# Sums of seven-product blocks ended in PSUM, and weight and word preparation moved between engines

## The chip, the core and the metric

The kernel runs on one core of one Trainium2 chip. The metric is device time in microseconds (us) of one execution. Before the change it is 1180.49 us, the median of three runs (1179.92, 1180.49 and 1183.63).

The names of the engines: PE is the matrix engine, DVE is VectorE, ACT is ScalarE, POOL is GpSimd, and SP is SyncE, which here issues nearly all DMAs. PSUM holds the results of matrix products in banks of 128x512 fp32 values, and SBUF everything else.

## The reference

Attention over 4 batches of 576 tokens, with 8 heads of 64, then two feed-forward blocks, all in float32:

```python
scores = (q_rot @ k_rot.T) / sqrt(64); attn = softmax(scores)
x = concat_heads(attn @ v)                                # 2304 x 512
x = (silu(x @ w_gate) * (x @ w_val)) @ w_out              # MoE1, d_ff 1536
out = (relu(x @ w_in2) ** 2) @ w_out2                     # MoE2, d_ff 2048
```

`q_rot` and `k_rot` are rotated by their positions. The weights arrive as 64-bit floats and are used with float32 accuracy.

## The kernel before

**Products.** Every matrix product is made of three products of rounded operands: each operand is split into a high part (ACT, L873, or a DVE cast) and the rest, its low part (a subtraction on POOL or DVE, L874), and PE adds high·high, high·low and low·high in PSUM (L1020). What the text calls a split is this pair of instructions.

**Tokens.** Each batch has 576 tokens. 512 of them form a block; the 64 left over of all four batches form a fifth block, the rest, of 256 tokens. Batches are worked in two pairs, (0,1) and (2,3).

**Seven products for eight.** For a pair, the up projections (gate, val, and `w_in2`) treat tokens and d_ff columns as a 2x2 block product and compute it with seven products (function `up`). They need seven words of the tokens (B11, T1, T2, B22, T3, B21, T4; the T words are differences of the batches) and seven weights of a 256-column group (four parts and four sums or differences, `combine`). Each of the seven products of one group is six 128x512 matmuls. Three partial results are copied from PSUM to SBUF by ACT (tiles `cp`), and three later ones are added to them by DVE into the SBUF tile (`cp<-q,cp`). The four results (1,1), (0,1), (0,0) and (1,0) then pass through the activation: in MoE1 a DVE instruction multiplies with the gate (`th<-th,cp`), in MoE2 one computes max(x,0)·x in place (`cp<-cp`). Each result is then split into a tile `h`, which the down projection (`down`) multiplies with `wo`; DVE adds its output to the accumulators (`acc<-d,acc`).

**Stages.** First attention, with the first two d_ff chunks of MoE1 of batches 0 to 2 as filler for PE (L780; outputs go through a tile `ys` to a buffer `ypart` in device memory, L807 and L808). Its end is also the start of the first two chunks of block 3 and the rest (`glu0`). Then MoE1 in five groups of 256 d_ff columns, for pair 0 with the rest, then for pair 1; then MoE2 in eight groups for pair 0 with the rest, and for pair 1. `down` is run once for each of these 26 groups.

**Weights.** A group's weights are loaded as 64-bit words (L378) and unpacked in `unpack`: ACT scales the high word, DVE shifts the low word (L893), and two DVE instructions with a shift and an OR (L881) build the fp32 word. In the feed-forward blocks all of these write SBUF tiles (`raw`, then `f` or `wf`). In the attention the same three instructions go through a PSUM tile `mm` (L384 to L386). `combine` makes the weight sums, four DVE instructions of 128x256 each (`f<-f`), and writes the group to device memory for pair 1. Then come the splits into `wi` and `wo`.

**Words.** Those of the first pair are made after the attention: tokens are read back from `xfull` (L870), DVE makes the differences (`tw`), and all seven words are split into the `xc` tiles. The words of the later pairs are written to device memory, read back by `fetch_x` and split.

**Order of the work.** Attention and filler are ordered by class `Plan` with rank numbers. The rest is listed in program order with the functions `dma`, `split`, `tt`, `stt`, `copy` and `mul` (L869 to L1023), and class `Order` (L214) schedules it: PE takes its products in the written order, every other instruction has a due time counted back from PE, and an engine takes the most urgent instruction that is ready in the plan. Where an instruction may run on two engines (a `split` with `free=True`), the plan chooses. The resulting order of each engine is fixed in the program. Buffers are rings of tiles of fixed length (`Ring`).

Of the kernel before, what the change touches and what calls it, by code (L numbers as in the profile page):

```python
# [213 lines left out]
class Order:  # L214


    HOP = 200
    LAND = 2000
    RATE = 310
    WINDOW = 4  # L220

# [3 lines left out]
    def add(self, ways, rd=(), wr=(), size=0):  # L225
# [28 lines left out]
        self.ops.append(dict(ways=ways, deps=deps, at=at, now=self.pe, size=size, stage=self.stage))  # L254

    def plan(self):
# [19 lines left out]
        free = dict.fromkeys(ready, True)  # L276
        issued, events, seq, moved, out = set(), [], 0, 0.0, []

# [5 lines left out]
        def make_ready(i):  # L284
            for e, _, _ in ops[i]["ways"]:
                heapq.heappush(ready[e], (ops[i]["stage"], place[i] if e == "PE" else ops[i]["late"], i))
# [5 lines left out]
        while events:  # L292
# [13 lines left out]
            for e, heap in ready.items():  # L306
                while heap and free[e]:
# [13 lines left out]
                    _, ns, fn = next(w for w in o["ways"] if w[0] == e)  # L321
                    o["eng"], o["start"], o["ns"] = e, now, ns
# [14 lines left out]
def tile_attention_moe_moe2(  # L337
# [65 lines left out]
    xfull = [tc.dram_tile([128, KT, S], F32, name=f"xfull{j}") for j in range(B)]  # L403

    w0 = [[None] * 3 for _ in range(NW)]
    with ExitStack() as p1:
# [336 lines left out]
        def add_spill(g):  # L743
            b, j = divmod(g, NP)
            xs = pair[g]["xs"]
            plan.add("SP", 450, lambda: nc.sync.dma_start(out=xfull[b][:, j], in_=xs()), [(xs, 0), (xs, 1)], [], g + 1 + rk("sp", g), size=294912)
# [76 lines left out]
        for b in range(NFB):  # L823
            add_filler(b)
        plan.places.update(places)
# [5 lines left out]
    HK = KT // 2  # L831
# [9 lines left out]
    def dram(shape, name, dtype=F32):  # L841
# [13 lines left out]
                h=Ring(6), th=Ring(4), thr=Ring(2), wf=Ring(1), wo=Ring(4), q=Ring(5), d=Ring(3),  # L855
                ys=Ring(3), h0=Ring(4), t0=Ring(2))
# [12 lines left out]
    def dma(dst, src, rd, wr, size, eng=None):  # L869
        od.add(("SP", 500, lambda: (eng or nc.sync).dma_start(out=dst(), in_=src())), rd, wr, size=size)  # L870

    def split(hi, lo, src, n, rd, whi, wlo, free=False):
        od.add(("ACT", act(n, 205), lambda: nc.scalar.activation(hi(), src(), AF.Copy)), rd, [whi])  # L873
        sub = lambda e: lambda: e.tensor_tensor(out=lo(), in0=src(), in1=hi().bitcast(F32), op=ALU.subtract)  # L874
        od.add([("Pool", gp(n), sub(nc.gpsimd))] + [("DVE", dve(n, 80), sub(nc.vector))] * free, rd + [whi], [wlo])

    def tt(out, a, b, op, n, rd, wr, extra=150):
        od.add(("DVE", dve(n, extra), lambda: nc.vector.tensor_tensor(out=out(), in0=a(), in1=b(), op=op)), rd, wr)  # L878

    def stt(out, a, x, b, op0, op1, n, rd, wr, extra=150):  # L880
        od.add(("DVE", dve(n, extra), lambda: nc.vector.scalar_tensor_tensor(out=out(), in0=a(), scalar=x, in1=b(), op0=op0, op1=op1)), rd, wr)  # L881
# [5 lines left out]
    def unpack(src, dst, wr):  # L887
# [5 lines left out]
        od.add(("DVE", 520, lambda: nc.vector.tensor_scalar(low(), low(), 29, None, ALU.logical_shift_right)), [], [(raw, 0)])  # L893
        stt(low, high, 3, low, ALU.logical_shift_left, ALU.bitwise_or, 512, [(raw, 1)], [(raw, 0)], 220)
        stt(dst, high, 0x80000000, low, ALU.bitwise_and, ALU.bitwise_or, 512, [(raw, 0), (raw, 1)], [wr], 220)
# [4 lines left out]
    def combine(w, c, keep):  # L900
# [5 lines left out]
        for out, x, y, op in ((4, 0, 1, ALU.add), (5, 4, 2, ALU.subtract), (6, 2, 0, ALU.subtract), (7, 3, 5, ALU.subtract)):  # L906
            tt(g(out), g(x), g(y), op, 256, [(f, x // 2), (f, y // 2)], [(f, 2 + (out - 4) // 2)], 80)
# [8 lines left out]
    def split_in(f):  # L916
        w = new("w")
        for d, n in PIECES:
            split(lambda d=d, n=n: w()[:, 0, d:d + n], lambda d=d, n=n: w()[:, 1, d:d + n], lambda d=d, n=n: f()[:, d + 1:d + 1 + n].bitcast(F32),
                  256 * n, [(f, (d + 1) // 2), (f, (d + n) // 2)], (w, (d, 0)), (w, (d, 1)), True)  # L920
# [13 lines left out]
    def split_out(f):  # L934
        w = new("wo")
        split(lambda: w()[:, 0], lambda: w()[:, 1], lambda: f().bitcast(F32), 512, [f], (w, 0), (w, 1), True)
        return w


    def words(get, put, parts=range(HK)):  # L940
        for i in parts:
            (b11, k11), (b12, k12), (b21, k21), (b22, k22) = get(i)
            t1, t2 = new("tw"), new("tw")
            tt(t1, b12, b11, ALU.subtract, 512, [k12, k11], [t1], 80)
            tt(b12, b22, b12, ALU.subtract, 512, [k22], [k12], 80)
            tt(t2, b22, t1, ALU.subtract, 512, [k22, t1], [t2], 80)
            put(T1, i, t1, t1)
            tt(t1, b21, t2, ALU.subtract, 512, [k21, t2], [t1], 80)
# [12 lines left out]

# [482 lines left out]
```

## Time and profile before

| | |
|---|---|
| median of three runs | 1180.49 us |
| the profiled execution's own time | 1183.9 us |
| its span in the profile | 1182.1 us |
| mean granted TensorE clock | 0.985 |
| PE busy | 1093.5 us, 93% |
| DVE busy | 925.4 us, 78% |
| ACT busy | 590.1 us, 50% |
| POOL busy | 566.4 us, 48% |
| matmuls | 6126 |

The span is what the profile records; the execution's own time is 1.8 us longer. The busy time of PE is a sum in which matmuls overlap in a pipeline, so a busy PE need not run at its best rate; what it could do at best is worked out from a stretch in which it never waits. The granted clock is a share of full speed, 2.4 GHz; at its lower level PE runs at 1.2 GHz.

### The profile page before, as it was taken

The numbers are of one execution on the slowest core, as the hardware profiler recorded it, in microseconds if no ns is written. First come the engines' busy times: TensorE is split into PE (matmuls) and PEld (weight loads), VectorE is DVE, ScalarE is ACT, GpSimd is POOL, SyncE is SP. The second block draws the span as 40 slices with busy tenths as digits, with TensorE's granted clock in tenths as the row PEclk, the third lists the DMA queues.
The fourth block names the chain that finished last, engine by engine and source line by source line (L and its number), as shares of the span: only waits on it lengthen the run. The fifth ranks groups of instructions, "written<-read, shape, count | busy, mean of one in ns | idle before, by whom it ended". The sixth has DMA issues, their size and how long they took to land.

```text
span 1182.1 us, 17248 instructions
## 1 busy us (share of the span) xinstructions
PE 1093.5 (93%) x6126; PEld 893.3 (76%) x6126; DVE 925.4 (78%) x1401; ACT 590.1 (50%) x1216; POOL 566.4 (48%) x410
## 2 busy tenths in 40 slices
PE   4899999999989799999978999979999998999998
PEld 3677887788867588877766777768778887877776
DVE  8777787677639699999989976796988868576675
ACT  7667676566525444543635444545343435643331
POOL 6886877564116254344555454462443426242321
PEclk9999999999999899999989999999999999999999
DMA  9756575655134553655667632362333425512001
GB/s 308 196 175 181 151 191 168 175 156 157 40 96 142 180 166 114 232 188 179 232 218 229 212 115 85 114 231 99 120 120 113 163 95 164 178 58 81 27 18 72
DMA packets 89861, 175.62 MB, mean 149 GB/s; under 512 B 16304, under 2 KB 42672, under 8 KB 89776
## 3 DMA queue, kind: packets, MB, share of 16 engines
q1 hardware_dynamic: 89088, 173.81, 46.8%
q8 instruction: 48, 0.79, 0.3%
q10 hardware_dynamic: 688, 0.72, 0.2%
q14 instruction: 37, 0.30, 0.1%
HBM read 105.97 MB, written 46.40 MB: 129 GB/s over the span
## 4 chain that ended last, share of the span: by engine, by line
PE 33%; DVE 15%; issue 2%; ACT 1%; POOL 1%; DMA 0%; DVEq 0%; POOLq 0%
PE d L1020 21%; PE q L1020 13%; DVE cp L878 3%; DVE cp L881 2%; DVE th L881 2%; DVE h L874 2%; DVE xc L874 1%; DVE acc L878 1%; DVE raw L881 1%; DVE f L878 1%; ACT h L873 1%; DVE tw L878 0%; DVE wi L874 0%; DMA raw<-in_moe_w_in_dram 0%; DVE raw L893 0%
## 5 line engine op out<-in xcount | busy, mean ns | idle before, releaser
L1020 PE MATMUL q<-xc,wi 128*128 128x512 f32 x1512 | 358.3, 393 | 13.4 <-DVE cp L878 8.7
L1020 PEld LDWEIGHTS q<-xc,wi 128*128 128x128 f32 x1512 | 282.4, 189 | 79.7 <-DVE cp L878 12.7
L874 POOL TENSOR_TENSOR wi<-f,wi 128x512 fp32r<-128x512 f32 (+1 forms) x115 | 158.7, 1387 | 150.9 <-ACT wi L873 144.2
L1020 PE MATMUL d<-wo,h 128*128 128x512 f32 (+1 forms) x870 | 208.8, 396 | 14.0 <-DVE thr L878 4.7
L1020 PEld LDWEIGHTS d<-wo,h 128*128 128x128 f32 x870 | 162.4, 190 | 57.2 <-DVE acc L878 7.6
L878 DVE TENSOR_TENSOR acc<-d,acc 128x512 f32<-128x512 f32 (+1 forms) x193 | 128.7, 683 | 49.0 <-PE d L1020 48.4
L1020 PE MATMUL d<-h,wo 128*128 128x512 f32 (+1 forms) x600 | 135.2, 381 | 17.1 <-DVE acc L878 12.9
L1020 PEld LDWEIGHTS d<-h,wo 128*128 128x128 f32 x600 | 106.4, 193 | 44.8 <-DVE acc L878 18.0
L874 POOL TENSOR_TENSOR wo<-wf,wo 128x512 fp32r<-128x512 f32 x38 | 54.4, 1431 | 151.7 <-ACT wo L873 144.2
L640 PE MATMUL s<-kh,qa 128*128 128x288 f32 x320 | 104.1, 350 | 21.2 <-DVE qa L598 12.3
L646 DVE TENSOR_REDUCE nm<-s 128x1 f32<-128x576 f32 x144 | 105.9, 751 | 16.1 <-PE s L640 14.6
L873 ACT ACTIVATE wi<-f 128x512 fp32r<-128x512 f32 (+1 forms) x144 | 80.4, 571 | 72.4 <-DVE f L881 29.6
L648 ACT ACTIVATE p<-s,nm 128x576 f32<-128x576 f32 x144 | 105.4, 734 | 16.1 <-DVE nm L646 14.2
L669 PE MATMUL pt<-ident,p 128*128 128x128 f32 (+1 forms) x720 | 109.2, 275 | 4.4 <-ACT pc L661 3.8
L878 DVE TENSOR_TENSOR cp<-q,cp 128x512 f32<-128x512 f32 x108 | 73.6, 685 | 40.2 <-PE q L1020 35.7
L884 ACT ACTIVATE cp<-q 128x512 f32<-128x512 f32 x108 | 64.0, 594 | 62.3 <-PE q L1020 61.0
L669 PEld LDWEIGHTS pt<-ident,p 128*128 128x128 f32 (+1 forms) x720 | 86.2, 135 | 10.7 <-ACT pc L661 4.7
L873 ACT ACTIVATE wo<-wf 128x512 fp32r<-128x512 f32 x52 | 32.7, 629 | 116.5 <-PE d L1020 75.3
L640 PEld LDWEIGHTS s<-kh,qa 128*128 128x128 f32 x320 | 60.3, 194 | 34.1 <-ACT p L648 14.9
L663 DVE COPY pc<-pt 128x512 f32<-128x512 f32 (+1 forms) x97 | 65.6, 686 | 25.0 <-PE pt L669 24.3
L640 PE MATMUL s<-kl,qz 128*128 128x288 f32 x288 | 84.8, 302 | 0.0
L703 PE MATMUL av<-pc,v 128*64 128x256 f32 x640 | 76.1, 384 | 0.0
(171 smaller groups left out, 1832.1 us busy)
## 6 DMA issues: line engine op xcount, KB each, us to landing
raw<-in_moe_w_out_dram SPq DMA_DIRECT2D x26, 512.0 KB, 3.9
w1d<-f SPq DMA_DIRECT2D x10, 896.0 KB, 3.7
f<-w1d SPq DMA_DIRECT2D x10, 896.0 KB, 5.1
f<-w2d SPq DMA_DIRECT2D x10, 896.0 KB, 4.6
rot<-in_k_dram SPq DMA_DIRECT2D x15, 576.0 KB, 4.7
rot<-in_q_dram SPq DMA_DIRECT2D x15, 576.0 KB, 3.8
kh<-rot SPq DMA_DIRECT2D x60, 144.0 KB, 2.6
raw<-in_moe_w_in_dram SPq DMA_DIRECT2D x16, 512.0 KB, 4.2
```

The costliest lines, as they stand in the source:

```text
L640: nc.tensor.matmul(ps()[:, i, :HS], lhsT=a, rhs=w, start=y == 0, stop=y == len(prods) - 1)
L646: plan.add("DVE", 755, lambda ps=ps, nm=nm: nc.vector.tensor_reduce(out=nm(), in_=ps()[:, :, :HS], axis=AX.XY, op=ALU.max, negate=True), [ ...
L648: plan.add("ACT", 930, lambda x=x, ps=ps, nm=nm, p=p: nc.scalar.activation(p().rearrange("p (a b) -> p a b", a=2), ps()[:, :, :HS], AF.Exp ...
L663: nc.vector.tensor_copy(dst()[:kk], pt()[:kk, :n])
L669: nc.tensor.matmul(pt()[:kk, off + n * 128:off + n * 128 + 128], lhsT=p()[:, c * 128:c * 128 + kk], rhs=ident, is_transpose=True)
L703: nc.tensor.matmul(av()[h * 64:h * 64 + 64, 0:256], lhsT=vt()[:, h, c], rhs=pcs[c]()[:, h * 256:h * 256 + 256], start=c == 0, stop=c == 4)
L873: od.add(("ACT", act(n, 205), lambda: nc.scalar.activation(hi(), src(), AF.Copy)), rd, [whi])
L874: sub = lambda e: lambda: e.tensor_tensor(out=lo(), in0=src(), in1=hi().bitcast(F32), op=ALU.subtract)
L878: od.add(("DVE", dve(n, extra), lambda: nc.vector.tensor_tensor(out=out(), in0=a(), in1=b(), op=op)), rd, wr)
L881: od.add(("DVE", dve(n, extra), lambda: nc.vector.scalar_tensor_tensor(out=out(), in0=a(), scalar=x, in1=b(), op0=op0, op1=op1)), rd, wr)
L884: od.add(("ACT", act(n), lambda: nc.scalar.activation(out(), src(), func, scale=scale)), rd, wr)
L1020: nc.tensor.matmul(ps(), lhsT=x, rhs=y, start=first and i == 0, stop=last and i == 2, skip_group_check=True)
```

## The change

It has five parts.

1. `up` ends its sums in PSUM: DVE adds the copied partial result from SBUF to the PSUM bank (`tt(Q, Q, r2)`) or into a new bank of ring `d`, and the activation reads PSUM. The order of the fourth and fifth product is exchanged. In MoE2 the square becomes an ACT ReLU into SBUF and a DVE product of that and PSUM. The rings are now q 3 (before 5), d 4 (before 3) and one bank p.
2. The unpacking of the weights in the feed-forward blocks goes through the PSUM bank p.
3. The first pair's words are made in the attention: their high and low parts are spilled as X is made (`xsp`), the four T words are subtracted, written, read back, split and written again (`add_words`, rank 1000), and after the attention 14 DMAs of 512 KB bring the words into `xc`, held until 12 us before their due time. `fetch_x` takes pair 1's B words from the spills too.
4. 64 of the 72 weight sums of 128x256 move from DVE to POOL (`tt_sb`); the low parts of `h`, `wi` and `wo` may only be made on POOL; word differences may go to POOL. The planner now counts that POOL and some DVE instructions hold each other up (`port`, `held`).
5. The rest's words are loaded with four DMAs before `glu0`; `down` cuts its outputs finer; the last group's splits in MoE1 pair 1 and MoE2 pair 0 come later (`later`, `finish`), with other orders of preparation there.

```diff
@@ up
-        product(R, w, S3, xc[T3], False)
-        tt(q1, R, q1, ALU.add, 512, [R], [q1])
-        yield (1, 1), q1
         product(Q, w, S4, xc[B22], False)
-        tt(r2, Q, r2, ALU.add, 512, [Q], [r2])
-        yield (0, 1), r2
-        T = new("q")
+        tt(Q, Q, r2, ALU.add, 512, [r2], [Q])
+        yield (0, 1), Q
+        product(R, w, S3, xc[T3], False)
+        U = new("d")
+        tt(U, R, q1, ALU.add, 512, [R, q1], [U])
+        yield (1, 1), U
+        T = new("d")
         product(T, w, A12, xc[B21], True)
-        tt(r1, T, r1, ALU.add, 512, [T], [r1])
-        yield (0, 0), r1
+        tt(T, T, r1, ALU.add, 512, [r1], [T])
+        yield (0, 0), T
@@ split_h, split_in, split_out
-        split(..., (h, 0), (h, 1), True)
+        split(..., (h, 0), (h, 1))
@@ relu_pair
-                    stt(x, x, 0.0, x, ALU.max, ALU.mult, 512, [], [x], 80)
-                hs[key] = split_h(x, x)
+                r = new("th")
+                copy(r, x, 512, [x], [r], AF.Relu)
+                tt(r, r, x, ALU.mult, 512, [x], [r])
+                hs[key] = put(r, r)
@@ combine
-            tt(g(out), g(x), g(y), op, 256, ...)
+            tt_sb(g(out), g(x), g(y), op, 256, ...)
+    def tt_sb(out, a, b, op, n, rd, wr, free=False):
+        ways = [("Pool", gp(n), fn(nc.gpsimd)), ("DVE", dve(n), fn(nc.vector))]
+        od.add(ways[1:] if od.stage == 0 else ways[:1 + free], rd, wr, port=True)
@@ unpack
+        p = new("p")
+        bits = lambda: p().bitcast(U32)
-        od.add(("DVE", 520, lambda: nc.vector.tensor_scalar(low(), low(), 29, ...
-        stt(low, high, 3, low, ...
-        stt(dst, high, 0x80000000, low, ...
+        od.add(("DVE", dve(512), lambda: nc.vector.tensor_scalar(bits(), low(), 29, ...
+        stt(bits, high, 3, bits, ...
+        stt(dst, high, 0x80000000, bits, ...
@@ add_spill
+            for i in range(2):
+                plan.add("SP", 450, lambda i=i: nc.sync.dma_start(out=xsp[b][i][:, j]..., in_=xbuf[b]()[i][:, j]...), ..., size=262144)
@@ down
-        for o in range(0, len(outs), 2):
+        cut = [0, *range(first, len(outs) + 1)]
+        for some in (outs[a:b] for a, b in zip(cut, cut[1:])):
@@ start of the feed-forward part
-    words(loaded(PAIRS[0], in_cp), put_here(xc))
+            fetch_spilled(xc[word], word, PAIRS[0])
+            dma(lambda ...: xc[word]()[:, h]..., lambda ...: xsum[...][:, 1 - h]..., [], ..., 524288, hold=True)
```

PE at the end of the attention, before the change; `pt` is a transpose of the last attention rows, `mm` the filler, and the rows of tile `q` are the first of `glu0`:

```order
L703 MATMUL av<-pc,v_110 64x256 x8
L703 MATMUL av<-pc_107,v_110 64x256 x2
L706 MATMUL av<-pcr,v_110 64x64 x10
L780 MATMUL mm<-h,w 128x512 x6
L725 MATMUL pt<-ident,rb 128x128 x2
L780 MATMUL mm<-h,w 128x512 x12
```

and now:

```order
L719 MATMUL av<-pc_123,v_126 64x256 x2
L722 MATMUL av<-pcr,v_126 64x64 x10
L820 MATMUL mm<-h,w 128x512 x6
L741 MATMUL pt<-ident,rb 128x128 x2
L820 MATMUL mm<-h,w 128x512 x18
L1064 MATMUL q_4789<-x3h,w 128x512
```

Behind the last transposes stand 18 filler matmuls, three steps of six, where there were 12, two steps.

DVE in MoE1 pair 0, at the preparation of a group, before the change; `accr` is the rest's accumulator, `f<-f` are the weight sums, `wi` a low part of a weight:

```order
L881 SCALAR_TENSOR_TENSOR raw_4654<-raw_4654 128x512
L878 TENSOR_TENSOR accr_4674<-d_4687,accr_4674 128x256
L881 SCALAR_TENSOR_TENSOR f_4658<-raw_4654 128x512
L878 TENSOR_TENSOR accr_4674<-d_4688,accr_4674 128x256
L878 TENSOR_TENSOR f_4658<-f_4658 128x256 x3
L878 TENSOR_TENSOR accr_4674<-d_4686,accr_4674 128x256
L878 TENSOR_TENSOR f_4658<-f_4658 128x256
L893 TENSOR_SCALAR raw_4653<-raw_4653 128x512
L874 TENSOR_TENSOR wi_4649<-f_4658,wi_4649 128x512
```

and POOL at the preparation of a group of the same stage now:

```order
L922 TENSOR_TENSOR f_4776<-f_4776 128x256 x3
L915 TENSOR_TENSOR wi_4766<-f_4776,wi_4766 128x256
L922 TENSOR_TENSOR f_4776<-f_4776 128x256
L915 TENSOR_TENSOR wi_4766<-f_4776,wi_4766 128x512 x2
L915 TENSOR_TENSOR wi_4767<-f_4777,wi_4767 128x512
L922 TENSOR_TENSOR f_4777<-f_4777 128x256 x3
L915 TENSOR_TENSOR wi_4767<-f_4777,wi_4767 128x256
L922 TENSOR_TENSOR f_4777<-f_4777 128x256
L915 TENSOR_TENSOR wi_4767<-f_4777,wi_4767 128x512 x2
L915 TENSOR_TENSOR wo_5115<-wf_5109,wo_5115 128x512
L915 TENSOR_TENSOR wo_5116<-wf_5109,wo_5116 128x512
L915 TENSOR_TENSOR h_5088<-th_5097,h_5088 128x512
```

The weight sums have left DVE and stand on POOL, between the weights' low parts and ahead of the next `h`.

POOL in MoE2 pair 1, before the change; `h` are low parts of a result, `wi` and `wo` of weights:

```order
L874 TENSOR_TENSOR wo_5015<-wf_5010,wo_5015 128x512
L874 TENSOR_TENSOR h_4990<-cp_4663,h_4990 128x512
L874 TENSOR_TENSOR h_4989<-cp_4662,h_4989 128x512
L874 TENSOR_TENSOR wi_4649<-f_4658,wi_4649 128x256
L874 TENSOR_TENSOR wo_5016<-wf_5010,wo_5016 128x512
L874 TENSOR_TENSOR wi_4648<-f_5021,wi_4648 128x512
L874 TENSOR_TENSOR wo_5017<-wf_5010,wo_5017 128x512
L874 TENSOR_TENSOR wi_4648<-f_5021,wi_4648 128x512 x2
L874 TENSOR_TENSOR wo_5014<-wf_5010,wo_5014 128x512
L874 TENSOR_TENSOR wi_4649<-f_4658,wi_4649 128x512
```

and now:

```order
L915 TENSOR_TENSOR wo_5116<-wf_5109,wo_5116 128x512
L915 TENSOR_TENSOR wi_4766<-f_4776,wi_4766 128x512
L915 TENSOR_TENSOR h_5088<-th_5097,h_5088 128x512
L915 TENSOR_TENSOR h_5089<-th_5098,h_5089 128x512
L915 TENSOR_TENSOR h_5090<-th_5099,h_5090 128x512
L915 TENSOR_TENSOR h_5091<-th_5100,h_5091 128x512
L915 TENSOR_TENSOR wi_4766<-f_4776,wi_4766 128x512
L915 TENSOR_TENSOR wi_4766<-f_4776,wi_4766 128x256
L915 TENSOR_TENSOR wo_5113<-wf_5109,wo_5113 128x512
L915 TENSOR_TENSOR wi_4767<-f_4777,wi_4767 128x512
L915 TENSOR_TENSOR wo_5114<-wf_5109,wo_5114 128x512
```

Of a group's four `h` two stood on POOL before; all four do now, one behind the other and behind the weights' low parts.

## Rows read from the trace of the kernel before

**Rows 1.** Busy time by stage: stretch, length, each engine's busy time (instructions), granted clock, DMA share, GB/s.

```profile
0.00:351.50 351.50, 319.35 (x2568) 264.12 (x2568) 250.03 (x448) 224.09 (x545) 210.78 (x159) 0.99 0.58 165
351.50:421.10 69.60, 58.27 (x277) 47.77 (x277) 53.96 (x69) 32.71 (x63) 33.12 (x22) 0.90 0.50 164
421.10:614.00 192.90, 177.96 (x888) 147.34 (x889) 184.81 (x278) 90.61 (x166) 90.46 (x67) 0.97 0.56 187
614.00:779.90 165.90, 154.38 (x662) 122.73 (x662) 137.06 (x179) 79.46 (x144) 85.59 (x56) 1.00 0.49 160
779.90:1007.50 227.60, 215.93 (x1009) 176.91 (x1009) 186.81 (x280) 101.50 (x191) 94.06 (x71) 0.99 0.42 139
1007.50:1182.20 174.70, 167.60 (x728) 134.38 (x726) 112.75 (x150) 61.70 (x109) 52.44 (x37) 1.00 0.21 68
351.50:1182.20 830.70, 774.14 (x3558) 629.13 (x3558) 675.39 (x953) 365.98 (x671) 355.66 (x251) 0.98 0.43 142
```

**Rows 2.** Chain that ended last, MoE2 pair 0: start us, us, what.

```profile
840.03 5.50 PE q L1020 x24
```

**Rows 3.** PE's waits, 351 to 1182 us: us in total, times, longest.

```profile
PE d L1020 <- DVE acc L878: 16.2, 15, 4.6
PE q L1020 <- DVE cp L878: 8.7, 7, 2.6
PE d L1020 <- DVE h L874: 7.1, 8, 2.8
PE d L1020 <- DVE thr L878: 4.7, 5, 2.1
PE q L1020 <- ACT cp L884: 4.4, 9, 0.8
PE d L1020 <- ACT xrd L873: 3.4, 1, 3.4
PE d L1020 <- POOL h L874: 3.2, 3, 1.2
```

**Rows 4.** DVE groups, 336 to 1182 us: count, busy us, mean ns, idle before and releaser.

```profile
L878 DVE TENSOR_TENSOR acc<-d,acc 128x512 f32<-128x512 f32 (+1 forms) x193 | 128.7, 683 | 49.0 <-PE d L1020 48.4
...
L881 DVE SCALAR_TENSOR_TENSOR th<-th,cp 128x512 f32<-128x512 f32 x60 | 64.6, 1093 | 0.3
L881 DVE SCALAR_TENSOR_TENSOR raw<-raw 128x512 uint32<-128x512 uint32 x62 | 56.7, 915 | 1.7 <-ACT raw L884 1.2
L881 DVE SCALAR_TENSOR_TENSOR cp<-cp 128x512 f32<-128x512 f32 x48 | 50.6, 1060 | 0.8
...
L878 DVE TENSOR_TENSOR f<-f 128x256 f32<-128x256 f32 (+1 forms) x74 | 39.6, 559 | 0.3
...
L874 DVE TENSOR_TENSOR h<-cp,h 128x512 fp32r<-128x512 f32 x27 | 24.6, 914 | 0.2
...
L878 DVE TENSOR_TENSOR tw<-acc,tw 128x512 f32<-128x512 f32 x8 | 8.8, 1103 | 0.2 <-DMA yd<-tw 0.2
```

**Rows 5.** DVE unpacking through PSUM, by form, 0 to 336 us, same columns.

```profile
L385 DVE SCALAR_TENSOR_TENSOR mm<-wa,mm 128x512 uint32<-128x512 uint32 x6 | 4.2, 694 | 0.2
```

**Rows 6.** POOL groups by form, 336 to 1182 us, same columns.

```profile
L874 POOL TENSOR_TENSOR wi<-f,wi 128x512 fp32r<-128x512 f32 x93 | 138.3, 1493 | 133.4 <-ACT wi L873 126.7 <-issue 3.9 <-PE d L1020 1.7
...
L874 POOL TENSOR_TENSOR h<-th,h 128x512 fp32r<-128x512 f32 x31 | 47.8, 1547 | 20.8 <-ACT h L873 20.6
...
L874 POOL TENSOR_TENSOR wi<-f,wi 128x256 fp32r<-128x256 f32 x22 | 20.6, 937 | 17.5 <-ACT wi L873 17.5
```

**Rows 7.** POOL by form, 0 to 336 us, where DVE uses mostly PSUM.

```profile
L798 POOL TENSOR_TENSOR h<-hf,h 128x512 fp32r<-128x512 f32 x6 | 7.7, 1278 | 20.3 <-ACT h L797 20.3
```

**Rows 8.** ACT by form, 336 to 1182 us.

```profile
L873 ACT ACTIVATE h<-th 128x512 fp32r<-128x512 f32 x56 | 35.0, 629 | 36.1 <-DVE th L881 35.5 <-DVE th L878 0.2
```

**Rows 9.** Timeline of ACT at the attention's end: start us, us, instruction, idle before and releaser.

```profile
346.90 0.60 ACT L807 ACTIVATE ys<-mm 128x512 f32<-128x512 f32 x1 [2.38 <-DMA ypart<-ys]
350.88 0.60 ACT L807 ACTIVATE ys<-mm 128x512 f32<-128x512 f32 x1 [3.38 <-DMA ypart<-ys]
```

More of the change, by code (lines that the diff above doesn't have):

```diff
@@ L220, with add @@
     WINDOW = 4
+    LEAD = 12000
     def __init__(self):
         self.ops, self.stage, self.pe = [], 0, 0
-    def add(self, ways, rd=(), wr=(), size=0):
+    def add(self, ways, rd=(), wr=(), size=0, port=False, hold=False):
         i = len(self.ops)
@@ L253, in add @@
             at, self.pe = self.pe, self.pe + ways[0][1]
-        self.ops.append(dict(ways=ways, deps=deps, at=at, now=self.pe, size=size, stage=self.stage))
+        self.ops.append(dict(ways=ways, deps=deps, at=at, now=self.pe, size=size, stage=self.stage, port=port, hold=hold))
     def plan(self):
@@ L276, in plan @@
         free = dict.fromkeys(ready, True)
+        held = {"DVE": 0, "Pool": 0}
         issued, events, seq, moved, out = set(), [], 0, 0.0, []
+        now = 0
         def at(t, *what):
@@ L284, in make_ready @@
         def make_ready(i):
+            o = ops[i]
+            if o["hold"] and now < o["late"] - self.LEAD:
+                at(o["late"] - self.LEAD, "ready", i)
+                return
             for e, _, _ in ops[i]["ways"]:
@@ L321, in plan @@
                     _, ns, fn = next(w for w in o["ways"] if w[0] == e)
+                    if e == "Pool" or e == "DVE" and o["port"]:
+                        ns += max(0, held["Pool" if e == "DVE" else "DVE"] - now)
+                        held[e] = now + ns
                     o["eng"], o["start"], o["ns"] = e, now, ns
@@ L824, in tile_attention_moe_moe2 @@
             add_filler(b)
+        for i in range(HK):
+            add_words(i)
         plan.places.update(places)
@@ L828, in tile_attention_moe_moe2 @@
                 fn()
-    HK = KT // 2
     BR = B * NR
@@ L1236, in down1 @@
         for b in (1, 0):
-            for o, _, ps, t in down(wo, [hs[i, b] for i in range(2)], [(o, ALL) for o in range(KT)], order=(b, 1 - b)):
+            for o, _, ps, t in down(wo, [hs[i, b] for i in range(2)], [(o, ALL) for o in range(KT)], first=1 + b):
                 a = acc[b][o]
@@ L1247, in tile_attention_moe_moe2 @@
             us, hs = {}, {}
+            last = g + 1 == G1
+            if p == g == 0:
+                ur = gate_rest(wg, xr)
             run(gate_pair(wg, xc, us))
-            if p == 0:
+            if p == 0 and g:
                 ur = gate_rest(wg, xr)
-            if held:
+            if held and not last:
                 down1(*held)
@@ L1301, in down2 @@
                 outs[3:] = [(3, slice(0, 256)), (3, slice(256, 512))]
-            for t, c, ps, key in down(wo, [hs[i, b] for i in range(2)], outs, tok=True, order=(b, 1 - b)):
+            for t, c, ps, key in down(wo, [hs[i, b] for i in range(2)], outs, tok=True, first=1 + b):
                 if g == 0:
```

276 lines of the change are left out of this document (164 added, 112 removed).

## The prediction

> **What bounds the kernel now.** I read the busy time by stage first [rows 1]. Behind the attention (0 to 351.5 us) come the start of the feed-forward part (to 421.1), MoE1 of pair 0 (to 614.0) and of pair 1 (to 779.9), and MoE2 of pair 0 (to 1007.5) and of pair 1. PE is the busiest engine in each but one: in MoE1 of pair 0 DVE is busy for 184.81 of 192.90 us, 96%, more than PE. Over the whole stretch from 351.5 us DVE has 675.39 of 830.70 us (81%) and POOL 355.66 (43%).
>
> Busy PE is not PE at its best, so I set a floor. In the chain of waits 24 matmuls of 512 columns take 5.50 us where PE waits for nothing [rows 2], 0.229 us each; half of it is taken for 256 columns. The program has 156 wide and 120 narrow matmuls in the start, 576 and 312 in the next stage, then 660 wide, 816 and 192, and 720 wide. The floors are 49.5, 167.6, 151.1, 208.8 and 164.9 us; against the lengths of the stages 20.1, 25.3, 14.8, 18.8 and 9.8 us are lost, 89 in all. The change leaves PE's matmuls as they are, so 89 us is the most that it can give behind the attention.
>
> What PE lost them to stands in its waits [rows 3]: an instruction of DVE ended waits of 16.2, 8.7, 7.1 and 4.7 us, 36.7 together, ACT's copies 4.4, the rest's word (xrd) 3.4, POOL's `h` 3.2. The granted clock took more: 0.90 of 69.60 us, 0.97 of 192.90 and 0.99 of 227.60 [rows 1] are 7.0, 5.8 and 2.3 us, 15 in all, in the stages where PE had idle time, and none in the two at 1.00. That is 36.7, 11 and 15; the other 26 are small waits and gaps.
>
> Why is DVE late? Its groups [rows 4] show two kinds of price. An instruction that reads PSUM takes 683 ns (`acc<-d,acc`). One of the same size with both inputs in SBUF takes 914 (`h<-cp,h`), 1060 (`cp<-cp`) or 1093 (`th<-th,cp`), and the POOL subtractions beside them take 1493 and 1547 [rows 6] where the same takes 1278 in the attention [rows 7]. So the two engines hold each other up when both read SBUF, and DVE pays most.
>
> **The change part by part.** *Sums in PSUM.* The multiplication with the gate now reads one input from PSUM: 60 x (1.093 - 0.683) = 24.6 us less DVE time; the square, 48 x (1.060 - 0.683) = 18.1 us less. ACT gets 48 more ReLU copies, at the 0.629 of the nearest row [rows 8] 30 us; ACT has 365.98 of 830.70 us now [rows 1], and only the last of a group's results has to wait for it. Ring `q` falls from five banks to three, but two uses go to `d`, which has four: a bank is held from its first product until the activation has read it. I price this at nothing, since the DVE instruction which frees the bank becomes faster; without that cover it is one DVE add, 0.7 us, per up projection.
>
> *Unpacking through PSUM.* The same instruction takes 915 ns on `raw` [rows 4] and 694 on `mm` [rows 5]: 62 x 0.22 = 13.7 us less. The one behind it, which writes the word, saves between nothing and as much; I take 9. In all 23.
>
> *Weight sums, low parts, words.* DVE loses 64 sums of 128x256, 64 x 0.559 = 36 us; 69 low parts of `h`, at 0.914 63 us; 29 wide and 14 narrow ones of weights, at 0.914 and half of it 33; 20 differences at 1.103 and 8 splits at 0.914, 29 [rows 4]. With the 66 above it loses 227 of 675 us and keeps 448.
>
> POOL gets about 54 wide low parts of `h`, 29 of weights and 12 differences less 12 splits, 83 at 1.278 = 106 us [rows 7]; and 15 + 14 + 64 narrow instructions at 0.80 (0.937 x 1.278 / 1.493 [rows 6, 7]), 74. It had 356; where DVE reads PSUM its old ones come down by up to 40 (93 x 0.215 of `wi` alone is 20). So 496 to 536 us, 63 to 68% of 785: under PE, but no longer idle.
>
> *First words in the attention.* The start has no DVE work for them and PE no wait for xrd. The attention pays: 16 more POOL instructions at 1.278, 20 us, on 210.78 of 351.50 busy; and 32 spills of 256 KB and 32 further DMAs on a DMA share of 0.58 [rows 1]. One more step of six filler matmuls stands behind the last transposes. Each such step waits there for the one `ys` tile: its copies start at 346.90 and 350.88, both after a DMA [rows 9], 4.0 us apart, of which its matmuls need 1.4 at 0.229. I take 4 us for the attention as a whole; between nothing (all behind PE's work) and 20 (all of POOL's new time on the path).
>
> *The sum.* Of the 36.7 us that DVE ended I take 28: a queue in front of the instruction goes, the instruction itself stays. Of the clock's 15, 9, as it fell only where PE idled. Of the words and copies xrd's 3.4 whole and half of ACT's 4.4. Of the 26 small ones 6. That is 48.6, less 4 in the attention: 44.6. The profiled execution took 1183.9 us, so 1139.3; it lay 3.4 us above the median of the runs, 1180.49, so **1136** on that scale. By stages it is about 9 us in the start, 16 in MoE1 of pair 0, 9 in that of pair 1, 10 in MoE2 of pair 0 and 2 in the last, where DVE has room already, less what the attention gives back.
>
> **The rivals.** *POOL late for `h` (slower).* Every low part of `h` now stands in POOL's one line with weight sums and weights. In MoE2 of pair 1 a result has an add 0.68, ReLU 0.63, product 0.68, high part 0.63 and low part 1.28 us on its way, with hops and another add in DVE's line about 5.1, while PE has four products of six matmuls, 5.5 us, before it needs the tile. From 0.4 us late it shows. Two other POOL instructions ahead make 2 x 1.28 - 0.4 = 2.2 us; once in each of 26 groups it is 57 us, and the time is 1136 + 57 = 1193. For it: POOL's `h` already ended 3.2 us of waits [rows 3] with less in the line. Against it: the rows of the new order put a group's `h` together, and POOL has a third of its time free. Chance 0.09. The Trainium skill ("GPSIMD Engine Reference", section 4.1, Engine selection) speaks against this move: an elementwise add on a tile belongs on VectorE, GpSimd being about twice as slow with two inputs. By that rule a weight sum should stay on DVE; that holds for its own duration, 0.80 against DVE's 0.559 beside POOL, and not for the load of the engines, which decides here.
>
> *DVE was only named last.* Its waits change names: ACT's copy and the three `q` banks end them instead. Then only MoE1 of pair 0, where DVE is full, gains its 16 us and the start 4, less 4: 1180.5 - 16 = 1164. For it: in MoE2 of pair 1 DVE has 112.75 of 174.70 us, and 10 us are lost all the same. Against: 36.7 us of waits name DVE in all stages. Chance 0.17.
>
> *The attention eats it.* All of POOL's 20 us lies on the path instead of 4: 1136 + 16 = 1152. This lies in the forecast's own range.
>
> *The floor is reached.* With nearly every wait gone 80 of the 89 are won: 1180.5 - 80 = 1100. Chance 0.07, since latency through three engines remains at each group.
>
> *It does nothing*, because the low parts are late for another reason (a DMA that brings weights): 1180. Against it: none of PE's larger waits is ended by a DMA [rows 3]. Chance 0.05.
>
> **How the numbers follow.** The forecast has 0.62, with 1118 to 1152 as its own range: 28 may be 15 or 33, 9 may be 4 or 13, the attention 0 to 20. The range of **1110 to 1168** takes in the relief of the full stage alone and half the way to the floor; outside are slower (0.09), nothing (0.05), and the far end of the floor. A difference of 0.3%, 3.5 us, is about what a measurement of this kernel can tell from no change. Faster by more than that has 0.62 + 0.17 + 0.07, **0.86**; within it **0.05**; slower **0.09**.
>
> **What would show it.** Right: in the profile after, DVE's busy time from the end of the attention near 450 us and POOL's near 500; the rows of `th` and of the square at about 0.68 us; PE's waits for DVE under 10 us; MoE1 of pair 0 near 177 us and the start near 61; the clock at 0.97 or more in the start. Wrong: PE's waits now ended by POOL's `h` or `wi`, several us in each stage (the slower rival); waits of the same size ended by ACT's `cp` (the second); an attention that ends after 360 us. What would make it wrong most easily is that a wait goes and the next one behind it, unseen now, has the same length.

## The result and the profile after

The changed kernel takes 1143.0 us (median of four runs, 1141.04 to 1145.25) against 1182.06 us of the kernel before on the same chips: a ratio of 0.9671, 95% interval 0.9643 to 0.9698. The forecast was 1136 us in a range of 1110 to 1168. The time is in the range, but the way to it is another, and the stages show that at once. The busy time by stage of the changed kernel (stretch, length, busy time of PE, PEld, DVE, ACT and POOL with instructions, granted clock, DMA share, GB/s), cut at the same matmuls as [rows 1]:

```profile
0.00:368.40 368.40, 325.77 (x2568) 266.09 (x2568) 255.09 (x449) 232.82 (x558) 223.61 (x169) 0.99 0.72 212
368.40:438.40 70.00, 53.39 (x276) 45.58 (x276) 31.16 (x51) 25.67 (x50) 20.91 (x18) 0.88 0.55 210
438.40:609.40 171.00, 169.30 (x889) 145.19 (x890) 132.27 (x217) 87.12 (x159) 124.92 (x120) 1.00 0.65 221
609.40:761.10 151.70, 150.56 (x662) 123.72 (x661) 101.47 (x153) 81.05 (x145) 108.29 (x91) 1.00 0.56 184
761.10:969.70 208.60, 208.60 (x1009) 175.96 (x1008) 141.71 (x217) 111.78 (x213) 140.81 (x130) 1.00 0.44 151
969.70:1139.30 169.60, 165.13 (x727) 135.20 (x726) 76.53 (x114) 73.67 (x134) 85.29 (x70) 1.00 0.21 67
368.40:1139.30 770.90, 746.99 (x3558) 625.64 (x3558) 483.14 (x749) 379.29 (x699) 480.22 (x427) 0.99 0.47 160
```

| stretch | before | after | change | forecast | floor |
|---|---|---|---|---|---|
| attention | 351.5 | 368.4 | +16.9 | +4 | |
| start | 69.6 | 70.0 | +0.4 | -9 | 49.5 |
| MoE1, pair 0 | 192.9 | 171.0 | -21.9 | -16 | 167.6 |
| MoE1, pair 1 | 165.9 | 151.7 | -14.2 | -9 | 151.1 |
| MoE2, pair 0 | 227.6 | 208.6 | -19.0 | -10 | 208.8 |
| MoE2, pair 1 | 174.7 | 169.6 | -5.1 | -2 | 164.9 |

The floors are the forecast's best lengths. Three stages came within 3.4 us of theirs (one lies 0.2 us below it, so a floor is not exact) and the last within 4.7. The four gave 60 us where 37 were forecast. The attention and the start together took 17 us of that back where they should have gained 5. Two errors nearly cancel.

PE's waits behind the attention (engine and what it waited for: us in total, times, longest), to be held against [rows 3]:

```profile
PE q L1064 <- ACT cp L930: 16.2, 2, 15.5
PE q L1064 <- ACT ys L847: 4.0, 1, 4.0
PE d L1064 <- ACT wo L914: 1.1, 1, 1.1
PE d L1064 <- DVE acc L919: 0.9, 1, 0.9
PE d L1064 <- POOL wo L915: 0.7, 1, 0.7
PE q L1064 <- DVE th L927: 0.5, 1, 0.5
PE d L1064 <- POOL h L915: 0.3, 1, 0.3
```

DVE ended 36.7 us of waits before and ends 1.4 now; POOL's `h`, the slower rival, 0.3. The larger waits that are left are two on ACT, 15.5 and 4.0 us, both in the first 48 us behind the attention.

The DVE groups from 353 us on (count, busy us, mean ns, idle before) answer to [rows 4]; `p` is the new PSUM bank of the unpacking:

```profile
L927 DVE SCALAR_TENSOR_TENSOR p<-raw,p 128x512 uint32<-128x512 uint32 x62 | 42.8, 690 | 1.7 <-ACT raw L930 0.8
...
L927 DVE SCALAR_TENSOR_TENSOR th<-th,q 128x512 f32<-128x512 f32 x40 | 27.3, 683 | 4.5 <-ACT th L930 2.7 <-PE q L1064 1.6
L927 DVE SCALAR_TENSOR_TENSOR th<-th,d 128x512 f32<-128x512 f32 x40 | 27.1, 682 | 1.0 <-ACT th L930 0.7
...
L919 DVE TENSOR_TENSOR th<-th,q 128x512 f32<-128x512 f32 x32 | 21.8, 681 | 2.4 <-ACT th L930 2.4
```

The unpacking's shift-and-or takes 690 ns on the PSUM bank (915 before), the gate's products 682 and 683 (1093) and the squares 681 (1060). Behind the attention DVE is busy for 483.14 us (675.39 before), and POOL for 480.22 (355.66). Two POOL groups by form, for [rows 6]:

```profile
L915 POOL TENSOR_TENSOR h<-th,h 128x512 fp32r<-128x512 f32 x104 | 136.2, 1336 | 101.0 <-ACT h L914 99.9 <-PE d L1064 0.9
...
L922 POOL TENSOR_TENSOR f<-f 128x256 f32<-128x256 f32 x64 | 46.9, 748 | 10.0 <-DVE f L927 9.8
```

POOL makes 104 low parts of `h` of full size now, and each is shorter, 1336 ns instead of 1547. A weight sum takes 748 ns on POOL. The Trainium skill ("GPSIMD Engine Reference", section 4.1, Engine selection) says that an add with two inputs is about twice as long on GpSimd. Beside POOL's own work DVE had needed 559 ns [rows 4], so here it is a factor of 1.3.

The attention ends 16.9 us later. At its end ACT copies the filler's outputs into the one tile `ys` (start us, us, instruction, idle before and releaser):

```profile
357.62 0.60 ACT L847 ACTIVATE ys<-mm 128x512 f32<-128x512 f32 x1 [2.49 <-DMA ypart<-ys]
362.08 0.60 ACT L847 ACTIVATE ys<-mm 128x512 f32<-128x512 f32 x1 [3.87 <-DMA ypart<-ys]
367.77 0.60 ACT L847 ACTIVATE ys<-mm 128x512 f32<-128x512 f32 x1 [5.09 <-DMA ypart<-ys]
```

The copies come 4.5 and 5.7 us apart, and one more than in [rows 9] stands behind the last transposes.

In the start the DMA engines are nearly full: from 376 to 414 us they are 97% busy at 368 GB/s.

```profile
376.00:414.00 38.00, 24.66 (x154) 21.98 (x153) 15.77 (x26) 12.89 (x26) 15.29 (x13) 0.89 0.97 368
```

In the chain of waits through this stretch (start us, us, what) nearly all of the time is DMAs:

```profile
378.36 8.46 DMA xc<-xsum
...
386.83 10.46 DMA xc<-xsum
...
397.35 9.66 DMA ypart<-ys
...
407.07 7.78 DMA ypart<-yh
```

And ACT's timeline shows where it ends:

```profile
414.96 0.66 ACT L930 ACTIVATE thr<-d 128x256 f32<-128x256 f32 x2 [18.72 <-DMA ypart<-yh]
415.50 1.09 ACT L930 ACTIVATE cp<-q 128x512 f32<-128x512 f32 x2
```

ACT had been idle for 18.72 us, until the store of `yh` had landed, which the trace names as what `thr` waited for. The copies of partial sums that PE waited for (`cp`) stand behind `thr` in ACT's line.

### The profile page after: what moved, and what is told of

Its sections match the earlier page's. It is cut to its first block, busy times and chain, and to the rows that moved or that the text cites. A ratio compares the mean times of both kernels' runs of the same rounds, so it can differ in the third digit from the quotient of the medians.

```text
span 1139.3 us, 17496 instructions
## 1 busy us (share of the span) xinstructions
PE 1072.8 (94%) x6126; PEld 891.7 (78%) x6126; DVE 738.2 (65%) x1198; ACT 612.1 (54%) x1257; POOL 703.8 (62%) x596
## 4 chain that ended last, share of the span: by engine, by line
PE 79%; DMA 9%; DVE 3%; SPq 3%; POOL 2%; ACT 2%; issue 1%; ACTq 0%; DVEq 0%; POOLq 0%
PE d L1064 36%; PE q L1064 26%; PE s L656 5%; PE av L719 5%; PE pt L685 4%; PE mm L820 3%; DMA qa<-rot 2%; DMA xc<-xsum 2%; DMA ypart<-ys 1%; SPq L636 1%; DMA v<-in_v_dram 1%; DMA h<-xfull 1%; POOL rot L566 1%; DVE nm L662 1%; DMA ypart<-yh 1%
## 5 line engine op out<-in xcount | busy, mean ns | idle before, releaser
L1064 PE MATMUL q<-xc,wi 128*128 128x512 f32 x1296 | 310.5, 392 | 16.7 <-ACT cp L930 16.2
L1064 PEld LDWEIGHTS q<-xc,wi 128*128 128x128 f32 x1296 | 242.5, 189 | 69.3 <-ACT cp L930 17.5
L915 POOL TENSOR_TENSOR wi<-f,wi 128x512 fp32r<-128x512 f32 (+1 forms) x144 | 167.1, 1176 | 70.2 <-ACT wi L914 64.5
L1064 PE MATMUL d<-wo,h 128*128 128x512 f32 (+1 forms) x870 | 199.9, 388 | 0.3 <-POOL h L915 0.3
L915 POOL TENSOR_TENSOR h<-th,h 128x512 fp32r<-128x512 f32 x104 | 136.2, 1336 | 101.0 <-ACT h L914 99.9
L919 DVE TENSOR_TENSOR acc<-d,acc 128x512 f32<-128x512 f32 (+1 forms) x193 | 132.1, 688 | 71.1 <-PE d L1064 66.8
L1064 PE MATMUL d<-h,wo 128*128 128x512 f32 (+1 forms) x600 | 126.1, 369 | 2.7 <-ACT wo L914 1.1
L915 POOL TENSOR_TENSOR wo<-wf,wo 128x512 fp32r<-128x512 f32 x52 | 68.0, 1307 | 78.9 <-ACT wo L914 41.4
L919 DVE TENSOR_TENSOR q<-q,cp 128x512 f32<-128x512 f32 x36 | 25.2, 699 | 105.5 <-PE q L1064 104.5
```

What stands on the lines that cost most here:

```text
L919: od.add(("DVE", dve(n), lambda: nc.vector.tensor_tensor(out=out(), in0=a(), in1=b(), op=op)), rd, wr)
L1064: nc.tensor.matmul(ps(), lhsT=x, rhs=y, start=first and i == 0, stop=last and i == 2, skip_group_check=True)
```

## The experiments

Theory A: the relief of DVE took the waits away, and the words made in the attention ("the early words") cost more than they save. Each run is compared with the kernel before on the same chip. The runs are on several chips, on which the kernel before took 1180.7 to 1182.4 us, so a microsecond or two between runs means nothing.

| kernel | us | ratio to before (95%) |
|---|---|---|
| as changed | 1143.0 | 0.9671 (0.9643 to 0.9698) |
| no_words | 1115.8 | 0.9431 (0.9404 to 0.9458) |
| spills_only | 1123.6 | 0.9497 (0.9457 to 0.9536) |
| store_act | 1139.0 | 0.9635 (0.9613 to 0.9657) |
| no_words_wv | 1113.0 | 0.9417 (0.9382 to 0.9453) |
| sums_sb | 1159.2 | 0.9799 (0.9769 to 0.9829) |
| unpack_sb | 1161.4 | 0.9806 (0.9746 to 0.9866) |
| pool_free | 1139.0 | 0.9635 (0.9604 to 0.9666) |
| sb_all | 1168.3 | 0.9883 (0.9856 to 0.9910) |
| sb_all_nw | 1139.5 | 0.9642 (0.9600 to 0.9683) |
| b_cuts | 1182.9 | 0.9998 (0.9983 to 1.0013) |
| b_port | 1154.7 | 0.9764 (0.9736 to 0.9792) |
| best | 1114.6 | 0.9413 (0.9371 to 0.9456) |

**The words behind the attention again (no_words).**

```diff
-            add_words(i)
-            (the two spills xsp of add_spill)
+    words(loaded(PAIRS[0], in_cp), put_here(xc), tw="c1")
```

> The first pair's words are made behind the attention again (no spills of the split tokens, no subtractions in the attention); all else stays as changed. Theory A: the parts that relieve DVE bring PE to its floor behind the start, and the words in the attention cost more than they save. The attention then ends at 352 to 357 us instead of 368.4, the wait of 15.5 us in the start is gone, the words cost up to 10 us of it, and the time is 1115 to 1128 us. Rival B: the early words are what makes the start short; without them DVE and POOL are full there again, it lasts as long as before (70 us), and the time is 1138 us or more.

1115.8 us: theory A's time, and B falls. (Without the spills pair 1's tokens are read back and split again too, as before the change.) The attention ends at 350.2 us, earlier than A had it, and the start takes 66.6 us with its words, less than the 70.0 without them. Its stretch, and that from 376 to 414 us (columns as above):

```profile
350.20:416.80 66.60, 55.01 (x277) 46.54 (x278) 48.42 (x65) 33.25 (x64) 37.47 (x27) 0.90 0.57 183
376.00:414.00 38.00, 28.12 (x132) 23.31 (x133) 28.20 (x38) 17.00 (x33) 20.20 (x15) 0.87 0.50 163
```

The DMA engines are half as busy there as in the changed kernel, and yet the start is only 3.4 us shorter. DVE, which makes words there now, is busy for 48.42 us of it, against 31.16. PE's waits (us in total, times, longest) from the attention's end on:

```profile
PE q L1070 <- ACT cp L925: 10.7, 4, 9.1
PE q L1070 <- ACT ys L844: 2.2, 1, 2.2
PE d L1070 <- POOL h L910: 2.0, 3, 1.3
PE q L1070 <- DVE th L922: 0.5, 1, 0.5
```

The wait of 15.5 us is gone, but one of 9.1 for the same copies has come. The third part of the change, taken back, is worth 27 us.

**What of it is the spills (spills_only).**

```diff
 no_words, and in add_spill:
+            for i in range(2):
+                plan.add("SP", 450, lambda i=i: nc.sync.dma_start(out=xsp[b][i][:, j]..., in_=xbuf[b]()[i][:, j]...), ...)
```

> The kernel with the words made behind the attention (no_words), plus the 32 spills of split tokens in the attention, 256 KB each, which nobody reads here. Of the 18 us by which the attention ends later with the words in it, theory F gives most to the spills (32 more DMAs in SP's line, 8.4 MB written where the DMA engines are already the fullest): the attention ends at 360 us or more, and the time is 1126 us or more. Theory G gives it to the making of the words (16 POOL instructions and 32 DMAs in a chain of load, subtract, write, read, split, write, in POOL's and SP's line ahead of the attention's own): the attention then ends by 354 us here, and the time is within 4 us of no_words, 1112 to 1120 us.

Neither theory: the attention ends at 357.5 us, between the two, and the time is 1123.6. PE's first matmul behind the attention (start us, us, instruction, idle before and releaser):

```profile
357.48 0.49 PE L1073 MATMUL q<-x3h,w 128*128 128x512 f32 x1 [2.59 <-ACT ys L847]
```

So of the 18.2 us by which it ends later with the words than without, the spills take 7.3 and the making of the words (POOL's work and the words' own DMAs, which no run separates) 10.9.

**The stores of block 3 from ACT (store_act).**

```diff
-        dma(lambda o=o: ypart[B - 1][:, o, :], lambda ys=ys: ys(), ..., 262144)
+        dma(lambda o=o: ypart[B - 1][:, o, :], lambda ys=ys: ys(), ..., 262144, nc.scalar)
```

> The four stores of block 3's first partial output (ypart from ys and yh) are issued by ACT, right behind the copy that fills each, instead of by SP behind the words' loads. Theory A: the 15.5 us in the start are a chain: the tile thr lies where yh lay, its first write waits for the store of yh, which stands in SP's line behind 14 loads of words and four of accumulators, and ACT's copies of partial sums stand behind thr. Then the wait falls below 5 us and the time is 1127 to 1134 us. Rival C: the DMA engines are full with the words (7.3 MB), and the seven products would wait for these anyway; the wait is then 10 us or more under another name, and the time 1138 us or more.

1139.0 us: by the time rival C. The wait of 15.5 us falls to 3.8, as theory A had it, but two others of 5.7 us together, for the copies into `ys`, are new:

```profile
PE d L1064 <- ACT ys L930: 5.7, 2, 3.7
PE q L1064 <- ACT cp L930: 4.4, 2, 3.8
```

The time is 4 us shorter than the changed kernel's, which the intervals of the ratios, overlapping, do not tell from none. The timeline of ACT:

```profile
396.02 0.60 ACT L930 ACTIVATE ys<-d 128x512 f32<-128x512 f32 x1 [6.55 <-DMA xc<-xsp]
...
412.25 0.66 ACT L930 ACTIVATE thr<-d 128x256 f32<-128x256 f32 x2 [7.15 <-DMA ypart<-yh]
```

ACT was idle for 6.55 us until a word's load had landed, with its own store as the next thing to issue, and ACT then waited for the store of `yh` until 412.25. So the order in SP's line alone was not the limit. From 376 to 414 us the DMA engines are 92% busy in this run too, which fits a limit there; what made ACT wait for a load of SP the trace does not show.

**The val weights later (no_words_wv).**

```diff
+    od.stage = 1
     wv = split_in(combine(w_val, NW, w1d[0][1]))
-    od.stage = 1
```

> The kernel with the words made behind the attention (no_words), and the first val weights prepared in the second list of the plan instead of the first, so that ACT's copies of the first partial sums don't stand behind their splits. no_words has one long wait left in the start, 9.1 us for such a copy. Theory H: the copy stands in ACT's line behind the val weights' high parts, which wait for DVE (words, unpacking and sums of the start together): the wait falls to 3 us or less and the time is 1106 to 1111 us. Rival: the words themselves are late, or the val weights come too late instead: 1114 us or more.

1113.0 us, between the two, and by the intervals level with no_words: the wait falls from 9.1 to 5.9, and 2.1 come back for a val weight.

```profile
PE q L1070 <- ACT cp L925: 6.6, 2, 5.9
...
PE q L1070 <- ACT wi L909: 2.1, 1, 2.1
```

Beside these waits the words are made, on DVE next to POOL (DVE: start us, us, instruction); that their making is what is left is argued, not shown:

```profile
372.07 1.77 DVE L917 TENSOR_TENSOR xw<-xw 128x512 f32<-128x512 f32 x1 [1.86 <-POOL xc L910]
...
377.51 1.78 DVE L910 TENSOR_TENSOR xc<-xw,xc 128x512 fp32r<-128x512 f32 x1
```

A 128x512 difference and a low part, both with two inputs in SBUF, take 1.77 and 1.78 us on DVE there, against 0.68 where one input is in PSUM. These are long ones: the eight differences take 1.34 us on average.

**All three reliefs undone (sb_all), and the words too (sb_all_nw).**

```diff
 up:      tt(q1, R, q1, ...); yield (1, 1), q1      (and r2, r1 likewise, in SBUF)
 squares: stt(x, x, 0.0, x, ALU.max, ALU.mult, ...)  (three of four)
 unpack:  in place in raw
 splits of h, wi, wo: free=True;  weight sums: tt(...)
```

> The three parts that relieve DVE are undone together: sums and squares end in SBUF, the unpacking goes through SBUF, the weight sums are on DVE and the low parts may go to DVE again. The words stay in the attention. Theory A: the waits for DVE come back, 50 to 65 us, on top of the words' cost: 1195 to 1208 us, slower than the kernel before. Rival D: most of the gain behind the start comes from the other orders and tile counts of the change, not from DVE's load: 1150 to 1170 us.

1168.3 us: rival D's range. But this kernel does not compute the reference's result, so its time is a hint only. Another experiment leaves out both, the reliefs and the early words:

> Both undone: the words are made behind the attention, and sums, unpacking, weight sums and low parts are as before the change (sums end in SBUF, no POOL-only work). What is left of the change is the finer cutting of the down projection's outputs, the banks (3, 4, 1), the order of two products, the rest's word, the later splits of two groups and the plan's count of the shared port. Theory A (DVE's load held PE): the waits for DVE are back, and the time is 1165 to 1185 us. Rival D (the orders and cuts did most of it, as the run with all three parts undone and the words kept, 1168 us, suggests): 1132 to 1150 us.

1139.5 us: rival D again, far from A. With the three reliefs undone (only 17 word differences stay on POOL), and with the words where they were, 42 us of gain remain. Between this run and no_words, which differ in the reliefs alone, lie 24 us: that is what the reliefs together are worth. The stretch from 440 to 1100 us (columns as above) says how full DVE is there, before the change and in sb_all_nw:

```profile
440.00:1100.00 660.00, 620.80 (x2862) 505.12 (x2861) 548.53 (x781) 302.94 (x556) 292.42 (x209) 0.99 0.46 151
440.00:1100.00 660.00, 642.66 (x3002) 529.73 (x3001) 567.53 (x770) 313.35 (x574) 366.34 (x258) 1.00 0.45 151
```

567.53 of 660 us, 86%, more than the 548.53 of before, and PE is idle (the stretch less its busy time) for 17 of 660 us where it was for 39. A full DVE by itself does not explain the time of before.

**One of them undone (sums_sb, unpack_sb, pool_free).**

> Only the sums of the seven products and the squares end in SBUF again (36 instructions of MoE1's gate pair and 48 squares read two inputs in SBUF). Theory A: what counts is DVE's load, and with the other two parts it stays under 65% of the time behind the attention, so little comes back: 1143 to 1152 us. Rival E: it is the latency of the sums that counted, each result passing the engines' shared port: the waits of PE for DVE return in each group, 26 times about 1 us, 1165 us or more.

> Only the unpacking goes through SBUF again; all else as changed. By the rows of before it is 62 x 0.37 = 23 us of DVE time, against 84 x 0.38 = 32 us of the sums, whose undoing cost 16 us. If DVE's load is what counts, the time rises in the same proportion, by 8 to 14 us, to 1151 to 1157 us; if only the latency of the sums counted, it stays within 4 us of 1143.

> The kernel as changed, with its early words, but the weight sums on DVE again and the low parts of h and of the weights free to go to DVE or POOL. By the rows this gives DVE 64 sums and about 90 low parts back, some 100 us at the lengths of before; the undoing of the sums in SBUF (16 us) and of the unpacking (18 us) gave it 30 and 23. Theory A (DVE's load): the most of the three, 1160 to 1170 us. Rival: the line of POOL was as much of a limit as DVE, and a free choice costs little or nothing: 1138 to 1150 us.

Each is one piece of the diff above: sums_sb its first two lines, unpack_sb the third, pool_free the fourth. They take 1159.2, 1161.4 and 1139.0 us. The sums cost 16, between the two theories; the unpacking 18, more than either, though its four runs lie between 1154 and 1166; and the move from DVE to POOL was worth nothing that can be measured: undone it is 4 us faster, with intervals that overlap, in the rival's range and not theory A's. The stretch from 440 to 1100 us, sums_sb and unpack_sb:

```profile
440.00:1100.00 660.00, 647.99 (x3048) 539.35 (x3048) 459.88 (x659) 318.58 (x580) 460.59 (x390) 0.99 0.47 160
440.00:1100.00 660.00, 643.05 (x3017) 534.75 (x3016) 460.13 (x656) 332.11 (x613) 471.94 (x392) 0.99 0.47 160
```

and pool_free, then the kernel as changed:

```profile
440.00:1100.00 660.00, 656.79 (x3120) 550.34 (x3119) 520.45 (x800) 339.34 (x631) 339.33 (x269) 1.00 0.47 160
440.00:1100.00 660.00, 657.86 (x3123) 551.14 (x3124) 431.37 (x667) 342.66 (x631) 446.56 (x400) 1.00 0.48 161
```

DVE is 70% busy in sums_sb and 79% in pool_free, and it is pool_free that lets PE work through: 656.79 us against 647.99. So DVE's load doesn't order them. I added up the work that takes all of its inputs from SBUF, POOL's instructions and DVE's with two inputs there, each with the length that it has where nothing holds it up (1.28 or 0.75 us on POOL, 0.68 or 0.41 on DVE): about 410 us of 660 in pool_free and 470 as changed, where PE is idle for 2 to 3 us; 523 in sums_sb, 538 in unpack_sb and 536 in sb_all_nw, where it is for 12 to 17. This is an estimate over five runs that differ in other things too; a run that changes this sum alone was not made. It is not the whole cause: the kernel before has about 497 and b_port (below) 514, and PE is idle for 39 and 27 us in them.

A rival is open. The plan takes an instruction of DVE on 512 columns for 0.68 us wherever its inputs lie (`dve(512)` in the kernel), and counts neither the gate's products nor the unpacking among those that POOL holds up. In sums_sb and unpack_sb they are longer than that:

```profile
L927 DVE SCALAR_TENSOR_TENSOR th<-th,cp 128x512 f32<-128x512 f32 x54 | 58.4, 1101 | 0.4
```

So part of the 16 and of the 18 us may be the order of a plan with wrong lengths, and no run separates it from the lengths themselves.

**Two other parts, alone on the kernel before (b_cuts, b_port).**

```diff
 b_cuts, in down:
-        for o in range(0, len(outs), 2):
+        cut = [0, *range(first, len(outs) + 1)]
+        for some in (outs[a:b] for a, b in zip(cut, cut[1:])):
 b_port, in Order.plan:
+                    if e == "Pool" or e == "DVE" and o["port"]:
+                        ns += max(0, held["Pool" if e == "DVE" else "DVE"] - now)
+                        held[e] = now + ns
```

> The kernel before with one thing of the change: the down projections take their outputs one by one (the first two together for b = 1), where they took them in pairs. In the run without the relief of DVE and without early words 42 us of gain are left, and this is the first candidate: the largest wait of before, 16.2 us, is PE in a down projection waiting for an accumulation, with two of three banks d bound by a pair. Theory I: it takes that wait away with DVE as full as it is, and the clock's loss with it: 1155 to 1168 us. Rival J: DVE only falls behind elsewhere, and the wait moves to another row: 1175 us or more.

1182.9 us, no change: rival J. No row of its profile is read here.

> The kernel before with one other thing of the change: the plan counts that a POOL instruction and a low part on DVE hold each other up, so the order of the engines and the share of low parts between POOL and DVE come out otherwise; the instructions are the same. Theory K: the old plan took DVE for faster than it is and so put the wrong work ahead: with true lengths 1150 to 1165 us. Rival J: the order matters little while DVE is 81% busy: 1174 us or more.

1154.7 us: theory K. The same instructions, planned with the knowledge that POOL and low parts on DVE hold each other up, are 28 us faster. The plan changes the order, and 16 of 389 low parts move from DVE to POOL. The larger of PE's waits for DVE in it:

```profile
PE q L1024 <- DVE cp L882: 6.0, 6, 1.8
PE d L1024 <- DVE h L878: 6.0, 4, 2.6
PE d L1024 <- DVE acc L882: 5.5, 10, 1.1
...
PE d L1024 <- DVE thr L882: 2.9, 4, 1.0
```

against 8.7, 7.1, 16.2 and 4.7 us in [rows 3]: 20.4 together, where it was 36.7. DVE is as busy as before, for 552.51 of 660 us:

```profile
440.00:1100.00 660.00, 633.38 (x2936) 518.08 (x2935) 552.51 (x781) 308.95 (x566) 323.23 (x228) 0.99 0.44 150
```

**A version that beats both (best).**

```diff
 no_words_wv, with the splits of h, wi, wo free=True and the weight sums on DVE, as in pool_free
```

> The words behind the attention, the first val weights in the second list, and the weight sums on DVE with the low parts free to go to DVE or POOL: the three edits that each were level or faster by themselves (1113 and 1139 us against 1143). Behind the start both parents lose almost nothing, so only the start can differ. Theory L (what costs is the time in which POOL and DVE instructions with two SBUF inputs keep each other out): this one has the smallest sum of such work of all, and the time is 1105 to 1113 us. Rival: in the start, where the words are made, every low part on DVE makes the words later: 1114 to 1120 us.

1114.6 us, level with no_words_wv (1113.0): the intervals of their ratios overlap. Theory L's range, up to 1113, is missed by 1.6 us and the rival's reached, though the work with all inputs in SBUF is the smallest here by the same estimate (about 408 us). Both beat the change by 28 to 30 us and the kernel before by 67 to 68.

## Why the prediction was right, and where it was not

*What bounds the kernel* held in its floor and its ceiling: 89 us could be won, and no_words, at 1115.8, wins 65 of them. Its next step failed: "Why is DVE late?" was answered with its load and its long instructions, and the gain was credited to their relief. The three reliefs together are worth 24 us (sb_all_nw against no_words), the other parts of the change 42 (sb_all_nw against before), and 28 come from the plan alone (b_port), with DVE as busy as before. The change's text showed the counting of the port in the plan, and no term of the sum had it. A low part that takes 914 ns on DVE where the plan of before expects 613 (`dve(n, 80)`) is not only long, it is out of place; this reading fits b_port, whose text differs from the kernel before only in that POOL and DVE wait for each other in the plan.

*Sums, squares and unpacking through PSUM* were priced right as lengths (0.683 and 0.694 forecast, 0.681 to 0.690 measured), and of the reliefs they are the parts that cost when undone.

*Weight sums and low parts to POOL.* DVE fell to 483 us, forecast 448, and POOL rose to 480, forecast 496 to 536. The lengths of DVE's instructions, added up from the trace, fell by 212 us (743 to 531), near the forecast 227; neighbours overlap, so its busy time fell by 192. That POOL would have room was right: its `h` ends 0.3 us of waits, and the slower rival did not come. But the move gains nothing (pool_free). The Trainium skill's rule ("GPSIMD Engine Reference", section 4.1, Engine selection), that an elementwise add belongs on VectorE, agrees with that as far as it goes: following it cost nothing here.

*"Of the 36.7 us that DVE ended I take 28", 9 of the clock's 15, 6 of the small 26*: the terms were mis-sized. In the four stages of the groups practically all of it went: the clock is 1.00 there and the lengths are near the floors. The rival that the floor is reached had 0.07, and in those stages it came. In the start it was the other way: the clock was to be 0.97 or more and is 0.88. The forecast's list by stages adds up to 46 us before the attention's 4 are taken off, where its terms add up to 48.6.

*"I take 4 us for the attention"* was mis-sized most: 16.9 as profiled, and the attention ends at 368.4, past the 360 that was named as a sign of being wrong. POOL's 20 us on the path are not the reason by themselves, since the spills, which need no POOL, cost 7.3 and the rest 10.9. The rival "the attention eats it" had about the amount. *The start* was to gain 9 us and gained nothing: that 14 loads of 512 KB come behind the attention, in the place of eight of 256 KB, was in the change and had no term in the sum. From 376 to 414 us 14 MB move at 368 GB/s, 7.3 MB of them these loads, and PE's wait of 15.5 us ends with a store that lands behind them.

So 60 us gained against 37 forecast, and 17 us given back against 5 gained: 43 in the profile against the forecast's 42 from the same stages, and the time came out right by luck: too little was expected of the groups, mostly for the wrong reason, and too little of what the early words would cost.

What stays open: sb_all_nw is 15 us faster than b_port, and which of the banks, the order of two products, the rest's word and the later splits give it was not tried. How much of the 24 us of the reliefs is DVE's time and how much the plan's order is open too.

## What to carry to other kernels

Where two engines hold each other up, the busier engine's share says little about the time, and the planner should have the lengths as they are under that holding: here this moved 28 us with no instruction changed and 16 on another engine. A step that is moved to an earlier stage to unload an engine must be priced with every byte that it writes and reads back, in the stage that it enters and at the hand-over: it was the dearest part of a change that gained all the same. Compare a forecast stage by stage; a sum that comes out right can hide two errors.

## What the runs showed of the hardware

DVE's 128x512 instructions with both inputs in SBUF took up to 1.78 us beside POOL in no_words_wv, 2.6 times the 0.68 with one input in PSUM. The Trainium skill ("SBUF — State Buffer", section "SBUF: two separate sides") says of the pair of SBUF ports that the two engines share that the instruction which starts first holds it for its whole length, and the other waits. The lengths fit that: 0.68 behind the whole of a POOL instruction of 1.28 would be 1.96 (an estimate), and 1.78 would be a wait for most of one.

Under a burst of loads a small store takes long to land: in the changed kernel, with the DMA engines 97% busy, the stores of 256 KB in the chain took 9.66 and 7.78 us. Issuing such a store from ACT did not free it of SP's loads: in store_act ACT stood for 6.55 us until a load of SP had landed, and the store of `yh`, issued at 406.28 us, landed 5.9 us later.
